# One load of the last head's values goes as three loads over 96, 20 and 12 rows

## The chip, the cores and the metric

The kernel runs on one core of a Trainium2 chip. The metric is the device time of one execution in microseconds. Before the change the median of three runs is 1369.03 us (1367.49 to 1369.67).

A core has engines that work side by side: TensorE (PE, with its weight loads as PEld), VectorE (DVE), ScalarE (ACT), GpSimd (POOL) and SyncE (SP). SP and ACT also issue DMAs. A DMA is carried out by up to sixteen DMA engines, which move its rows from the chip's memory (HBM) into the on-chip memory of 128 rows (partitions).

## The reference, cut to what matters

One token goes through two layers of attention over a long cache, each followed by a small MLP:

```
x = x + attention(layernorm(x))     # 32 heads, 8192 cached keys and values of 128 numbers
x = x + mlp(layernorm(x))           # 640 -> 1728 -> 640
x = x + attention(layernorm(x))     # the same cache and weights once more
x = x + mlp(layernorm(x))

q = x @ wq                          # per head: scores = q . k * 128**-0.5
p = softmax(scores);  o = p @ v     # over 8192 keys, then @ wo
```

Keys and values are float32: 4 MB of keys and 4 MB of values per head, 268 MB in all. Both layers read the same cache.

## The kernel before

The host lays keys and values out in one long array, `kv`, in the order in which they are read. A head is cut into units (`UNITS`, lines 41 to 53), each of which is one DMA. Most heads have two units, all keys and all values, of 4096 KB each. The heads at the ends of the layers are cut finer. Heads 0 and 31 have the units `HALVES[:2] + LAST`: two of keys with 2048 KB each, then four of values: blocks 0 and 1 (2048 KB, unit number 2), block 2 (1024 KB), three rows of block 3 (768 KB) and its last row (256 KB).

All units go through a ring in on-chip memory, 3496 x 8 numbers per row and 128 rows. `pump` (line 122) takes the next unit of the list `todo`, asks `place` (line 109) for room, and issues its load on SP (line 132). Where there is no room it stops, and is called again each time `release` (line 157) has freed a piece that was used. So loads go out in a fixed order, and each waits on SP until the instructions that read its place before are through. A unit of 2048 KB is 128 rows of 16 KB, one for each partition, and lies in `kv` row by row.

The first layer (0 in the code) goes through heads 0 to 31, the second (1 in the code) through heads 31 to 0. The ring still holds the last units of head 30 and all of head 31 when the first layer ends; the second layer starts with these and doesn't load them again. Four further units of the second layer are loaded into buffers that the first layer has just finished with (`load_beside`, line 142, on SP).

For a head PE makes the scores from the keys (`scores`, line 365), DVE takes their maximum (line 377), ACT the exponentials (line 384), PE turns them (line 392), and PE multiplies them by the values (`values`, line 426). Then the head's output is put together (`output`, line 440) and goes into the projection. Other small work of the layer is put between the pieces of a head by `side_work`: projections, queries of the next heads, and products of weights with weights.

In the last head of a layer the order matters most. Its keys' scores are mixed with the first MLP product (`hidden`, line 581). Values of blocks 0 and 1 come first, then another part of `hidden`, then blocks 2 and 3, then `output`. After that comes what remains of the MLP (`mlp`, line 759), which needs the head's output at once (line 762). In the first layer the loads beside and the next layer's start follow from it, in the second the result's store.

The DMAs of SP and ACT signal their end on semaphores, which the program hands out in turn. An instruction that reads a unit waits for the semaphore of its load.

Of the kernel before, what the change touches and what calls it, by code (L numbers as in the profile page):

```python
# [15 lines left out]
P = 128  # L16
# [34 lines left out]
] + HALVES[2:]  # L51
UNITS[28] = [("k", K_ALL[:1]), ("k", K_ALL[1:2])] + HALVES[1:]
UNITS[31] = HALVES[:2] + LAST
BESIDE = 4
DROPPED = {30: BESIDE}
RING = 3496
# [5 lines left out]
def wide(kind, piece):  # L62

    return 4 * piece[2] * (1 if kind == "k" else DH) // 8


def size(unit):
    return sum(wide(unit[0], piece) for piece in unit[1])
# [10 lines left out]
def decode_kernel(ctx: ExitStack, tc: tile.TileContext, x, kv, wq, wo, w1, w2, out):  # L79
    nc = tc.nc  # L80
# [12 lines left out]
    ring = consts.tile([P, 8 * RING], F32, name="ring")  # L93
# [5 lines left out]

    beside = todo[len(order) : len(order) + BESIDE]  # L100
    del todo[len(order) : len(order) + BESIDE]
    dram_at, o = {}, 0
# [6 lines left out]
    def place(layer, n):  # L109


        step = max(m for m in (8, 256, 512) if n % m == 0)
        low, high = (0, RING) if layer else ((3072, RING) if n == RING - 3072 else (0, 3072))
        at, best = low, None
        for a, m in sorted(live.values()) + [(high, 0)]:
            a = min(a, high)
            if a - at >= n and (best is None or a - at < best[1]):
                best = at, a - at
            at = max(at, -(-(a + m) // step) * step)
        return None if best is None else best[0]  # L120

    def pump():
        while todo:
            layer, u = todo[0]
            kind, pieces = unit = UNITS[u[0]][u[1]]
            n = size(unit)
            at = place(layer, n)
            if at is None:
                return
            todo.pop(0)  # L130
            o = dram_at[u]
            nc.sync.dma_start(
                ring[:, 8 * at : 8 * (at + n)],
                kv[o : o + 8 * P * n].rearrange("(p m) -> p m", p=P),
            )
            for t, piece in enumerate(pieces):
                m = wide(kind, piece)
                live[layer, u, t] = at, m
                at_of[layer, u, t] = ring, 8 * at
                at += m  # L140
# [16 lines left out]
    def release(L, u, t):  # L157
        if (L or u not in kept) and at_of[key(L, u, t)][0] is ring:
            del live[key(L, u, t)]
            pump()  # L160
# [23 lines left out]
    nc.sync.dma_start(xr, x)  # L184
    load_wq(0, nc.sync)
    pump()
    load_wo(0, nc.sync)

# [805 lines left out]
```

## Time and profile before

| | |
|---|---|
| median of the runs | 1369.03 us |
| the profiled execution, its own time | 1367.16 us |
| its span, first to last instruction | 1365.4 us |
| PE busy | 1009.0 us (74%) |
| DVE busy | 182.8 us (13%) |
| ACT busy | 113.2 us (8%) |
| bytes moved by DMA | 572.70 MB, 419 GB/s over the span |
| mean granted TensorE clock | 0.806 |

The span counts from the first to the last instruction; the execution's own time also has what lies around it. "Busy" sums the time in which an engine worked. The DMA share of a stretch is the mean busy share of the sixteen DMA engines. In a timeline row the two first numbers are start and duration in us, then come the engine, the line, the operation, what it writes and reads, and how many instructions are merged; a bracket names the idle time before the first of them and what ended it. A row of a windows table has the stretch, its length, the busy time (and instructions) of PE, PEld, DVE, ACT and POOL, the granted clock, the DMA share and the GB/s.

### The profile page before, as it was taken

The page shows a single profiled execution, that of the slowest core. Times are in us where ns is not written, and L with a number is a line of the kernel's source. Part 1 is how long each engine was busy: PE and PEld are TensorE (multiplying, and loading weights), DVE is VectorE, ACT ScalarE, POOL GpSimd, SP SyncE. Part 2 cuts the span into 40 slices and gives each one's busy share as a digit, 9 for nine tenths or more (in the row PEclk, how much of TensorE's full clock was granted, in tenths as well). Part 3 has the DMA queues.
Part 4 walks back from the last instruction along what each step waited for, and adds up shares of the span by engine and source line. Part 5 has one row for each costly group of instructions (what it writes and reads, how often), then busy time and mean ns, then how long its engine had stood idle before and what let it go on. Part 6 is the DMA issues. An engine that isn't in the chain of part 4 may idle for free.

```text
span 1365.4 us, 16727 instructions
## 1 busy us (share of the span) xinstructions
PE 1009.0 (74%) x7546; PEld 409.8 (30%) x7546; DVE 182.8 (13%) x696; ACT 113.2 (8%) x305; POOL 2.9 (0%) x10
## 2 busy tenths in 40 slices
PE   5564766877787777787888767676777787787778
PEld 2121312322333323343344322232222322223224
DVE  1010100111101101111122111110110101111112
ACT  0000000000101101111000100010100000000000
POOL 0000000000000000000000000000000000000000
PEclk9786867887878877888799987787788877787879
DMA  9999999999999999999979999999999999999995
GB/s 393 431 435 428 431 429 427 431 429 433 429 432 430 425 434 428 434 430 418 426 298 395 433 433 429 429 429 431 432 429 432 426 432 430 433 426 430 431 427 218
DMA packets 28736, 572.70 MB, mean 419 GB/s; under 512 B 3189, under 2 KB 3321, under 8 KB 5625
## 3 DMA queue, kind: packets, MB, share of 16 engines
q1 hardware_dynamic: 23912, 525.27, 90.0%
q10 hardware_dynamic: 4752, 46.37, 8.1%
q8 instruction: 59, 0.97, 0.3%
q14 instruction: 13, 0.10, 0.0%
HBM read 571.62 MB, written 0.00 MB: 419 GB/s over the span
## 4 chain that ended last, share of the span: by engine, by line
DMA 66%; PE 30%; DVE 2%; ACT 1%; issue 1%; SPq 0%; POOLq 0%; POOL 0%; ACTq 0%; DVEq 0%
DMA ring<-in_kv 66%; PE outs L426 11%; PE ps L365 10%; PE px L505 2%; PE pt L392 1%; ACT p L384 1%; PE px L311 1%; DVE h_t L377 1%; PE acc L581 1%; PE acc L331 1%; PE pm L412 1%; PE pm L452 1%; PE px L558 1%; PE px L538 0%; PE px L550 0%
## 5 line engine op out<-in xcount | busy, mean ns | idle before, releaser
L365 PE MATMUL ps<-ring,spread_q 128*32 128x512 f32 (+2 forms) x2064 | 319.9, 735 | 175.6 <-DMA ring<-in_kv 175.5
L426 PE MATMUL outs<-ring,pT 128*4 128x512 f32 (+2 forms) x2128 | 333.2, 776 | 47.0 <-DMA ring<-in_kv 46.7
L365 PEld LDWEIGHTS ps<-ring,spread_q 128*32 128x32 f32 x2064 | 62.0, 128 | 291.5 <-DMA ring<-in_kv 183.8
L426 PEld LDWEIGHTS outs<-ring,pT 128*4 128x4 f32 x2128 | 57.5, 101 | 255.1 <-issue 193.7
L377 DVE TENSOR_REDUCE h_t<-ps 128x1 f32<-128x512 f32 x64 | 44.3, 692 | 473.8 <-PE ps L365 473.6
L452 PE MATMUL pm<-h_t,p 128*128 128x1 f32 (+1 forms) x512 | 69.9, 258 | 34.6 <-DVE p L443 34.3
L452 PEld LDWEIGHTS pm<-h_t,p 128*128 128x128 f32 x512 | 64.6, 194 | 98.2 <-DVE p L443 97.2
L384 ACT ACTIVATE p<-ps,h_t 128x512 f32<-128x512 f32 x63 | 43.3, 687 | 578.7 <-DVE h_t L377 567.4
L392 PE MATMUL pt<-row_of,p 128*128 128x16 f32 x512 | 68.2, 265 | 22.7 <-ACT p L384 22.6
L443 DVE COPY p<-outs 128x256 f32<-128x256 f32 x62 | 26.3, 425 | 355.4 <-PE outs L426 355.4
L392 PEld LDWEIGHTS pt<-row_of,p 128*128 128x128 f32 x512 | 62.1, 191 | 34.6 <-ACT p L384 34.4
L405 PE MATMUL pm<-ident,h_t 128*128 128x128 f32 x128 | 31.1, 324 | 40.2 <-DVE h_t L377 40.2
L444 ACT COPY p<-outs 128x256 f32<-128x256 f32 x62 | 23.1, 372 | 454.5 <-DVE p L443 454.5
L505 PE MATMUL px<-w_t,wct 128*128 128x448 f32 (+1 forms) x80 | 46.8, 672 | 0.2 <-DVE wqc L527 0.2
L405 PEld LDWEIGHTS pm<-ident,h_t 128*128 128x128 f32 x128 | 19.0, 187 | 92.0 <-DVE h_t L377 89.6
L412 PE MATMUL pm<-h_t 128*128 128x1 f32 x128 | 27.7, 285 | 24.6 <-DVE h_t L409 24.6
L311 PE MATMUL px<-wq_t,ln_xc 128*32 128x128 f32 x630 | 31.1, 362 | 1.9 <-DMA wq_t<-in_wq 1.9
L311 PEld LDWEIGHTS px<-wq_t,ln_xc 128*32 128x32 f32 x630 | 26.7, 150 | 16.5 <-issue 13.6
L412 PEld LDWEIGHTS pm<-h_t 128*128 128x128 f32 x128 | 22.2, 217 | 30.8 <-DVE h_t L409 30.8
L331 PE MATMUL acc<-wo_t,o_cols 128*32 128x160 f32 x496 | 28.1, 382 | 0.0
L331 PEld LDWEIGHTS acc<-wo_t,o_cols 128*32 128x32 f32 x496 | 20.4, 144 | 18.7 <-issue 14.9
L505 PEld LDWEIGHTS px<-w_t,wct 128*128 128x128 f32 x80 | 13.9, 219 | 37.6 <-issue 36.5
(151 smaller groups left out, 344.3 us busy)
## 6 DMA issues: line engine op xcount, KB each, us to landing
ring<-in_kv SPq DMA_DIRECT2D x104, 4096.0 KB, 25.2
ring<-in_kv SPq DMA_DIRECT2D x29, 2048.0 KB, 23.0
wo_t<-in_wo ACTq DMA_DIRECT2D x14, 1280.0 KB, 17.5
wq_t<-in_wq ACTq DMA_DIRECT2D x13, 1280.0 KB, 17.3
ring<-in_kv SPq DMA_DIRECT2D x15, 1024.0 KB, 24.0
w_t<-in_w ACTq DMA_DIRECT2D x1, 4480.0 KB, 24.7
w_t<-in_w ACTq DMA_DIRECT2D x1, 4320.0 KB, 25.3
ring<-in_kv SPq DMA_DIRECT2D x3, 768.0 KB, 27.1
```

Of the source, the lines that this page charges most:

```text
L311: nc.tensor.matmul(pq[32 * j : 32 * j + 32, :DH], xc[:, c : c + 1].to_broadcast([P, 32]), weights_of(g, c, j), start=(c == 0), stop=(c == ...
L331: nc.tensor.matmul(acc[32 * g : 32 * g + 32, :DR], col.to_broadcast([col.shape[0], 32]), wt[:, g * DR : (g + 1) * DR], start=first, stop=last,
L365: nc.tensor.matmul(hd.ps[32 * g : 32 * g + 32, c : c + n], spread_q[:, 3 - r : 35 - r], tile_of[:, at + g * n : at + (g + 1) * n], start=f ...
L377: nc.vector.tensor_reduce(hd.nm, hd.ps, AX.X, ALU.max, negate=True)
L384: nc.scalar.activation(hd.p, hd.ps, AF.Exp, bias=hd.nm, scale=scale, accum_out=hd.l)
L392: nc.tensor.matmul(pt[:, 16 * b : 16 * b + 16], hd.p[:, b * P : (b + 1) * P], row_of.rearrange("p g r -> p (g r)"), start=True, stop=True,)
L405: nc.tensor.matmul(pt[:, :P], hd.nm.to_broadcast([P, P]), ident, start=True, stop=True)
L412: nc.tensor.matmul(pt[:, :1], hd.l.to_broadcast([P, P]), hd.wi, start=True, stop=True)
L426: nc.tensor.matmul((hd.out if r0 < 3 else hd.out_3)[32 * g : 32 * g + 4, r0:r1].rearrange("p r d -> p (r d)"), hd.pT[:, 4 * i : 4 * i + 4] ...
L443: nc.vector.tensor_copy(oc[:, :2], hd.out[:, :2])
L452: nc.tensor.matmul(pt[:, :n], oc[:, r], hd.w[:, r : r + 1].to_broadcast([P, n]), start=(r == 0), stop=(r == 3),)
L505: nc.tensor.matmul(pt[:, :n], wct[:, c], w1_t[:, c, f : f + n], start=(c == 0), stop=(c == NB - 1),)
```

## The change

The load of unit 2 of head 31 in the first layer, and of unit 2 of head 0 in the second, is issued as three DMAs one after the other on SP. They cover the partitions 0 to 95, 96 to 115 and 116 to 127. The bytes, their place in `kv` and their place in the ring stay the same, and so do all other loads. The instructions that read the unit now depend on three DMAs.

```diff
+UNEVEN = [(31, 2), (0, 2)]
+SHARES = [(0, 96), (96, 116), (116, 128)]
...
-            nc.sync.dma_start(
-                ring[:, 8 * at : 8 * (at + n)],
-                kv[o : o + 8 * P * n].rearrange("(p m) -> p m", p=P),
-            )
+            for p0, p1 in SHARES if u == UNEVEN[layer] else [(0, P)]:
+                nc.sync.dma_start(
+                    ring[p0:p1, 8 * at : 8 * (at + n)],
+                    kv[o + 8 * p0 * n : o + 8 * p1 * n].rearrange("(p m) -> p m", p=p1 - p0),
+                )
```

## The prediction

> **What bounds the kernel now.** The page comes first: its span, its queues, and the chain of waits.
>
> ```profile
> span 1365.4 us, 16727 instructions
> DMA  9999999999999999999979999999999999999995
> ...
> q1 hardware_dynamic: 23912, 525.27, 90.0%
> ...
> q8 instruction: 59, 0.97, 0.3%
> ...
> DMA 66%; PE 30%; DVE 2%; ACT 1%; issue 1%; SPq 0%; POOLq 0%; POOL 0%; ACTq 0%; DVEq 0%
> ...
> ring<-in_kv SPq DMA_DIRECT2D x29, 2048.0 KB, 23.0
> ```
>
> The stream of keys and values bounds the kernel: the sixteen DMA engines are full but for two slices, the layer's border and the end. The changed load lies just ahead of each of these. One row of it, 16 KB, costs an engine 0.900 x 16 x 1365.4 us over 525.27 MB / 16384 B (32060 rows), so 0.613 us. I call this a row time. The same load is now eight row times per engine, 4.9 us.
>
> The second view is the windows at the end of the second layer, and the timeline beside them.
>
> ```profile
> core 0: us, PE busy (x) PEld busy (x) DVE busy (x) ACT busy (x) POOL busy (x), PEclk, DMA share, GB/s
> 1341.00:1345.00 4.00, 3.38 (x32) 1.04 (x36) 0.12 (x1) 0.00 (x0) 0.00 (x0) 1.00 0.99 411
> 1345.00:1347.00 2.00, 2.00 (x23) 0.89 (x15) 0.69 (x1) 0.78 (x2) 0.00 (x0) 1.00 0.82 339
> 1347.00:1349.00 2.00, 1.62 (x16) 1.29 (x18) 0.76 (x5) 0.29 (x1) 0.00 (x0) 1.00 0.58 242
> 1349.00:1351.00 2.00, 2.00 (x40) 0.99 (x36) 0.28 (x1) 0.00 (x0) 0.00 (x0) 1.00 0.46 189
> 1351.00:1352.00 1.00, 1.00 (x22) 0.50 (x18) 0.00 (x0) 0.00 (x0) 0.00 (x0) 1.00 0.24 84
> 1352.00:1353.00 1.00, 1.00 (x25) 0.37 (x15) 0.08 (x1) 0.00 (x0) 0.00 (x0) 1.00 0.00 0
> ```
>
> The engines don't finish together. The first fall silent at about 1345 and the last at 1352, and for 4 us (1347 to 1351) about half of them run. What is left at 1345 is 0.82 x 2 + 0.58 x 2 + 0.46 x 2 + 0.24 = 4.0 us of all sixteen, so evenly shared rows would land 3 us earlier. The halves differ by about 5 us, which is eight row times. Half as many engines move about half the bytes (189 GB/s at 0.46, 411 at 0.99): each runs at its own pace, and silence of the others doesn't speed it.
>
> ```profile
> 1348.68 0.11 PEld L426 LDWEIGHTS outs<-ring,pT 128*4 128x4 f32 x8
> 1348.68 1.91 PE L426 MATMUL outs<-ring,pT 128*4 128x384 f32 x32
> ...
> 1351.12 1.94 PE L426 MATMUL outs<-ring,pT 128*4 128x384 f32 x32
> ...
> 1351.77 0.35 PEld L426 LDWEIGHTS outs<-ring,pT 128*4 128x4 f32 x12 [0.19 <-issue]
> 1352.51 0.25 PEld L426 LDWEIGHTS outs<-ring,pT 128*4 128x4 f32 x8 [0.40 <-DMA ring<-in_kv]
> ```
>
> PE takes the changed unit (blocks 0 and 1 of the last head's values) at 1348.68 without a wait, and the rest of the head from 1351.12. Only the last eight weight loads wait, 0.40 us against 0.19 by issue alone, and the matmuls hardly notice: 1.94 us for 32 against 1.91. So PE and the last bytes arrive together. An earlier landing is worth at most 0.03 us here. A later one has a little cover: those last matmuls are 8 x 128 of the group's 16 x 384 + 16 x 128 columns, 0.24 us. They end at 1353.06, so they start at 1352.82, 0.3 us after their weights.
>
> The first layer ends alike:
>
> ```profile
> 699.00:701.00 2.00, 1.62 (x19) 1.29 (x22) 0.82 (x5) 0.30 (x1) 0.00 (x0) 1.00 0.57 230
> 701.00:703.00 2.00, 2.00 (x40) 0.93 (x36) 0.22 (x1) 0.00 (x0) 0.00 (x0) 1.00 0.49 200
> 703.00:705.00 2.00, 2.00 (x37) 0.93 (x29) 0.14 (x1) 0.00 (x0) 0.00 (x0) 1.00 0.21 83
> ```
>
> ```profile
> 700.62 1.91 PE L426 MATMUL outs<-ring,pT 128*4 128x384 f32 x32
> ...
> 703.06 1.94 PE L426 MATMUL outs<-ring,pT 128*4 128x384 f32 x32
> ...
> 704.35 0.35 PEld L426 LDWEIGHTS outs<-ring,pT 128*4 128x4 f32 x8 [0.29 <-DMA ring<-in_kv]
> ...
> 706.93 0.94 PE L581 MATMUL acc<-mix,c_ol 128*32 128x448 f32 x8 [0.25 <-DVE c_ol L459]
> ```
>
> Half of the engines run for 4 us, and the last weights come 0.4 us ahead of their matmuls (705.00 - 0.24 - 704.35). The output of the head, the mixed weights (line 762) and the next layer's first loads hang on these matmuls, so a delay here passes on whole.
>
> **The change part by part.** *Rows per engine.* How many engines share a load can be counted in the queues. The first answer is a stretch with one load of 128 rows on queue 10, the second is the last 3 us, which hold only the store of four rows.
>
> ```profile
> q10 hardware_dynamic: 144, 1.31, 17.4%
> ...
> wo_t<-in_wo ACTq DMA_DIRECT2D x1, 1280.0 KB, 17.2
> ```
>
> ```profile
> q1 hardware_dynamic: 8, 0.00, 0.4%
> ...
> out<-xr SPq DMA_DIRECT2D x1, 2.5 KB
> ```
>
> 128 rows make 144 packets, 128 and 16 end marks; four rows make 8, four and 4 marks. So engines take equal shares, up to sixteen of them. Then 96 rows go six each; 20 rows go two each on ten engines (more can't share them evenly) and 12 rows one each on twelve; at the least four engines serve each, as with the store. If both begin at the same engine, ten engines get 6 + 2 + 1 = 9 rows, two get 7 and four get 6, where all had 8. [...]
>
> *What that moves, if a row keeps its price.* Eight engines are late and only six get lighter, so two late ones at least take a ninth row: the last landing moves between -0.61 us (two early ones among the late take it) and +0.61. Behind the cover of 0.3 and 0.4 us, PE loses up to 0.3 + 0.2 us in the two layers; a gain ends at 0.03 in each. I take +0.3 us together.
>
> *What a row costs in the new loads.* Until now every load covers the same 128 rows in the same shares, so the trace can't say whether the 0.613 us belongs to the engine or to the rows it writes. It does say that the engine isn't all: queue 8 brings 16 KB of instructions to another place in 0.003 x 16 x 1365.4 / 59 = 1.1 us (0.9 to 1.3 by the rounding of 0.3%). If rows own the lanes, sixteen lanes of eight rows, then the new loads crowd them. With neighbouring rows in a lane, rows 0 to 95 lie in twelve lanes: eight row times there instead of six. Rows 96 to 115 lie in 2.5 lanes, and 116 to 127 in 1.5: up to eight row times each, while twelve engines stand in line. From above that is 8 + 8 + 8 - 8 = 16 row times, +9.8 us, when nothing overlaps. From below, the early engines pass through each lane before the late ones arrive (they are eight row times ahead), and only the ninth row is left, +0.6 us. Nothing in the trace is nearer to one end, so I take the middle, +5.2 us in each layer. Less the cover that is 4.9 and 4.8, together +9.7 us.
>
> [...]
>
> *Issue and waits.* Two more issues in each layer:
>
> ```profile
> 1324.63 1.37 SPq L132 DMA_DIRECT2D ring<-in_kv  x3
> ```
>
> ```profile
> 684.70 0.11 PEld L426 LDWEIGHTS outs<-ring,pT 128*4 128x4 f32 x8 [3.42 <-DMA ring<-in_kv]
> ...
> 693.96 0.33 SPq L146 DMA_DIRECT2D wqc<-in_kv  x1
> ```
>
> ```profile
> 1332.77 0.11 PEld L426 LDWEIGHTS outs<-ring,pT 128*4 128x4 f32 x8 [1.98 <-DMA ring<-in_kv]
> ```
>
> Three issues take SP 1.37 us, so two more are 0.9 us, 20 us before the data is needed; the stream queued ahead hides them. The program hands its loads eight semaphores in turn, so a load waits for the eighth before it. The last small load will now wait for the last values of the head before, which land by 1332.77 (684.70 in the first layer), instead of going out by 1326. The earliest engine runs dry only at 1345, 12 us later; without that cover the cost would be the delay, 7 us. Behind it on SP stand the loads of line 146 in the first layer, the first of which goes out at 693.96 anyway, and in the second layer the store at the end. PE waits for three loads rather than one ahead of line 426. In the plain case they land before 1348.68, and the checks are at 0 to 0.1 us.
>
> The sum is 1367.16 us (the profiled execution's own time; its span is 1365.4) + 9.7 = 1376.9. The median of the runs shown is 1.87 us above that execution, so 1369.03 + 9.7 = 1378.7 us.
>
> **The rivals.** *Engines own the lanes.* Then the time is 1369.03 + 0.3 = 1369.3 us, no change. For it speaks that each engine keeps its pace when half are silent; against it, the 1.1 us of the instructions. It is the rival on the other side. It decides where a row in the new loads still takes 0.61 us.
>
> *Few engines.* If 20 and 12 rows go on four engines each, these take 6 + 5 + 3 = 14 rows, six more: +3.7 us, less the cover 3.4 and 3.3, so 1375.7 us. The store's four marks allow it; equal shares over sixteen speak against it.
>
> *Relief.* The 1.87 us between profiled and other executions could be waits for the late engines at both ends. If two rows less (1.2 us a layer) reached PE whole, the time would be 1369.03 - 2.4 = 1366.6 us. It decides only if PE in those runs waits over 0.6 us at each end for the last bytes, and if at most the two earliest of the eight late engines get a ninth row; here it waits 0.03.
>
> **How the numbers follow.** A measurement of this kernel tells about 0.2%, 2.7 us, from no change. Crowded lanes get 0.56: the trace leaves both owners open, and the price of instructions leans to the place written. Of this 0.52 is over 2.7 us and 0.04 under. Few engines get 0.06, all slower. Engine lanes get 0.32, no change. Relief gets 0.06, 0.04 of it faster and 0.02 within. So 0.58 slower, 0.38 the same, 0.04 faster. The likeliest case alone reaches from 1372 us to its upper bound, 1369.03 + 19.6 - 0.7 = 1388 us. The range of 8 in 10 takes in the engine lanes, 1367.5 to 1384 us.
>
> **What would show it.** Queue 1 has 23912 packets. With 16, 10 and 12 marks a layer has 22 more, 23956 in all; with 16, 4 and 4 it is 23928. Crowded lanes show as a DMA share near 1 with far fewer GB/s than 411 between 1340 and 1355 and around 700, the last weight loads of line 426 waiting some 5 us, and the first of them (at 1348.68 now) waiting too. Engine lanes show the same 411 GB/s, and a share that falls from 0.99 to 0 in 6 to 8 us. The forecast falls if both ends keep their 1.94 us matmul groups. The few-engine case shows a long tail at a share of about 0.25.

## The result, and the profile after

The changed kernel takes 1388.97 us (median of five runs, 1386.55 to 1393.16) against 1368.12 us before on the same chip (1367.49 to 1369.67). The ratio is 1.0148, with a 95% interval of 1.0136 to 1.0161. The forecast was 1378.7 us and the range ended at 1384.0 us: the direction was right, and the loss is more than twice the size.

From the page of the changed kernel: span, DMA activity in 40 slices, queues, and the chain of waits.

```profile
span 1384.7 us, 16734 instructions
DMA  9999999999999999999979999999999999999995
GB/s 394 432 430 433 426 430 432 430 426 431 431 430 431 430 429 432 428 425 425 399 193 402 428 433 431 427 431 430 434 430 428 429 432 428 433 431 430 430 410 129
...
q1 hardware_dynamic: 23956, 525.27, 90.2%
...
q8 instruction: 59, 0.97, 0.3%
...
DMA 70%; PE 26%; DVE 2%; ACT 1%; issue 0%; SPq 0%; POOLq 0%; POOL 0%; ACTq 0%; DVEq 0%
```

Queue 1 moves the same 525.27 MB with 44 packets more. The time of its packets rises from 0.900 x 1365.4 to 0.902 x 1384.7 us of each of the sixteen engines, so by 20.1 us (give or take 1 us by rounding). That is as much as the whole loss: the bytes are the same, and their transfer has become dearer.

The windows show where. Here is the end of the first layer, after (columns: stretch, length, busy time and instructions of PE, PEld, DVE, ACT and POOL, granted clock, DMA share, GB/s).

```profile
680.00:685.00 5.00, 4.62 (x24) 2.15 (x28) 0.83 (x5) 0.00 (x0) 0.00 (x0) 0.50 1.02 433
685.00:690.00 5.00, 3.68 (x28) 1.34 (x23) 0.58 (x2) 0.37 (x1) 0.00 (x0) 0.91 1.08 344
690.00:695.00 5.00, 3.55 (x34) 1.29 (x34) 0.33 (x2) 0.00 (x0) 0.00 (x0) 0.77 0.95 200
695.00:700.00 5.00, 3.24 (x28) 1.52 (x28) 0.38 (x2) 0.00 (x0) 0.00 (x0) 0.50 1.05 231
700.00:705.00 5.00, 4.04 (x22) 1.17 (x26) 0.00 (x0) 0.00 (x0) 0.00 (x0) 0.50 0.95 200
705.00:710.00 5.00, 4.40 (x36) 2.37 (x28) 1.44 (x5) 1.07 (x3) 0.00 (x0) 0.86 0.91 219
```

The end of the second layer, after, in the same columns:

```profile
1341.00:1345.00 4.00, 1.47 (x16) 0.32 (x16) 0.00 (x0) 0.00 (x0) 0.00 (x0) 0.96 1.02 434
1345.00:1350.00 5.00, 3.87 (x24) 2.07 (x20) 0.58 (x2) 0.37 (x1) 0.00 (x0) 0.50 1.08 324
1350.00:1355.00 5.00, 4.49 (x36) 1.91 (x28) 0.72 (x4) 0.00 (x0) 0.00 (x0) 0.50 0.97 208
1355.00:1360.00 5.00, 3.14 (x16) 0.63 (x20) 0.00 (x0) 0.00 (x0) 0.00 (x0) 0.50 0.99 225
1360.00:1365.00 5.00, 5.00 (x43) 2.13 (x35) 0.95 (x2) 0.78 (x2) 0.00 (x0) 0.83 0.99 212
```

For some 20 us at each end all sixteen engines are busy (DMA share 0.91 to 1.05) and move half of what they did: 200 to 231 GB/s where the first stretch of each table has 433 and 434. That is another picture than the tail of the kernel before, where half of the GB/s went with half of the share (189 GB/s at 0.46). At half pace a stretch of 20 us moves what 10 us would.

What PE sees of it, in the timelines. Before, the last keys and the matmul that follows the head's end:

```profile
694.50 1.06 PE L365 MATMUL ps<-ring,spread_q 128*32 128x512 f32 x8
1342.56 0.16 PEld L365 LDWEIGHTS ps<-ring,spread_q 128*32 128x32 f32 x8 [1.14 <-DMA ring<-in_kv]
1354.98 0.94 PE L581 MATMUL acc<-mix,c_ol 128*32 128x448 f32 x8 [0.25 <-DVE c_ol L459]
```

After, the same places and the values between them (the lines of the code stand four further down):

```profile
700.96 1.94 PE L369 MATMUL ps<-ring,spread_q 128*32 128x512 f32 x8 [2.21 <-DMA ring<-in_kv]
711.14 1.91 PE L430 MATMUL outs<-ring,pT 128*4 128x384 f32 x32 [1.36 <-issue]
715.10 1.06 PE L430 MATMUL outs<-ring,pT 128*4 128x384 f32 x16 [0.45 <-DMA ring<-in_kv]
718.09 0.94 PE L585 MATMUL acc<-mix,c_ol 128*32 128x448 f32 x8 [0.25 <-DVE c_ol L463]
...
1358.57 1.94 PE L369 MATMUL ps<-ring,spread_q 128*32 128x512 f32 x8 [1.77 <-DMA ring<-in_kv]
1367.05 1.91 PE L430 MATMUL outs<-ring,pT 128*4 128x384 f32 x32 [0.73 <-DMA ring<-in_kv]
1371.00 1.09 PE L430 MATMUL outs<-ring,pT 128*4 128x384 f32 x16 [0.44 <-DMA ring<-in_kv]
1374.02 0.95 PE L585 MATMUL acc<-mix,c_ol 128*32 128x448 f32 x8 [0.25 <-DVE c_ol L463]
```

The matmul of `hidden` that follows the head starts at 718.09 in place of 706.93 us in the first layer, 11.2 us later. In the second it starts at 1374.02 in place of 1354.98, 19.0 us later, of which 7.9 us are new. The span grows by 19.3 us. The delay reaches PE in part ahead of the changed unit: the last keys, an unchanged load, come 6.5 us later in the first layer (694.50, 700.96), and 4.8 us on top of the first layer's delay in the second (1342.56, 1358.57). Between the keys and the values PE itself is slower too: eight matmuls of scores take 1.94 us where they took 1.06, with a granted clock of 0.50 in place of 1.00. The end isn't set by that, as the last sixteen matmuls of the values still wait for a DMA in both layers (0.45 and 0.44 us).

### The profile page after: what moved, and what is told of

Read it like the earlier page. It is cut to its first block, busy times and chain, and to the rows that moved or that the text cites. A ratio compares the mean times of both kernels' runs of the same rounds, so it can differ in the third digit from the quotient of the medians.

```text
span 1384.7 us, 16734 instructions
## 1 busy us (share of the span) xinstructions
PE 1021.4 (74%) x7546; PEld 413.9 (30%) x7546; DVE 182.6 (13%) x696; ACT 113.2 (8%) x305; POOL 2.9 (0%) x10
## 3 DMA queue, kind: packets, MB, share of 16 engines
q1 hardware_dynamic: 23956, 525.27, 90.2%
## 4 chain that ended last, share of the span: by engine, by line
DMA 70%; PE 26%; DVE 2%; ACT 1%; issue 0%; SPq 0%; POOLq 0%; POOL 0%; ACTq 0%; DVEq 0%
DMA ring<-in_kv 70%; PE outs L430 10%; PE ps L369 9%; PE px L509 2%; PE pt L396 1%; ACT p L388 1%; DVE h_t L381 1%; PE px L562 1%; PE acc L335 1%; PE pm L416 1%; PE px L315 1%; PE px L554 0%; PE pm L456 0%; DVE pT L404 0%; PE pt L335 0%
## 5 line engine op out<-in xcount | busy, mean ns | idle before, releaser
L430 PE MATMUL outs<-ring,pT 128*4 128x512 f32 (+2 forms) x2128 | 338.7, 788 | 55.5 <-DMA ring<-in_kv 53.9
L396 PE MATMUL pt<-row_of,p 128*128 128x16 f32 x512 | 71.8, 273 | 21.9 <-ACT p L388 21.6
L396 PEld LDWEIGHTS pt<-row_of,p 128*128 128x128 f32 x512 | 65.6, 200 | 33.9 <-ACT p L388 33.8
```

What stands on the lines that cost most here:

```text
L396: nc.tensor.matmul(pt[:, 16 * b : 16 * b + 16], hd.p[:, b * P : (b + 1) * P], row_of.rearrange("p g r -> p (g r)"), start=True, stop=True,)
L430: nc.tensor.matmul((hd.out if r0 < 3 else hd.out_3)[32 * g : 32 * g + 4, r0:r1].rearrange("p r d -> p (r d)"), hd.pT[:, 4 * i : 4 * i + 4] ...
```

## The experiments

The theory is the prediction's own: a lane into the on-chip memory belongs to the rows written there, and loads of neighbouring rows crowd the lanes. The lanes are the author's assumption and stand in no view; the runs can only test what would follow from them. The rivals: what an additional load or wait costs by itself, the uneven shares of the engines, the place that is read, and for the size of the loss, whether it goes by the bytes that are split or by the distance between early and late engines. The ratios are against the kernel before on the same chip, with 95% intervals; a loss in us is the ratio's excess times 1368 us. The edits are to the changed kernel, and some show only the lines that matter.

### Three loads, no rows split

`cols` cuts the same unit into three loads by columns: each covers all 128 rows, and the bytes are as with 96, 20 and 12 rows.

```diff
+COLUMNS = [(0, 3072), (3072, 3712), (3712, 4096)]
-            for p0, p1 in SHARES if u == UNEVEN[layer] else [(0, P)]:
+            for c0, c1 in COLUMNS if u == UNEVEN[layer] else [(0, 8 * n)]:
                 nc.sync.dma_start(
-                    ring[p0:p1, 8 * at : 8 * (at + n)],
-                    kv[o + 8 * p0 * n : o + 8 * p1 * n].rearrange("(p m) -> p m", p=p1 - p0),
+                    ring[:, 8 * at + c0 : 8 * at + c1],
+                    kv[o : o + 8 * P * n].rearrange("(p m) -> p m", p=P)[:, c0:c1],
                 )
```

> The same two loads (unit 2 of the last heads) go as three loads each, cut by columns (12288, 2560 and 1536 bytes of each row) instead of by rows: all 128 rows in each, so every engine keeps its own eight rows. Lanes owned by rows: nothing is crowded, 1368.1 us within 0.5 us. Cost of the extra loads themselves (their issue, end marks, semaphores and the waits on them): all of the loss stays, 1386 to 1391 us.

Measured 1368.93 us against 1368.33, a ratio of 1.0003 (0.9994 to 1.0013). Two more issues, waits and end marks cost nothing that shows; cutting by rows does.

### One layer alone

```diff
-UNEVEN = [(31, 2), (0, 2)]
+UNEVEN = [(31, 2), None]        # first
+UNEVEN = [None, (0, 2)]         # second
```

> The three loads by rows in the first layer only. Lanes owned by rows: the loss of the first layer alone, by the later time of its last matmuls about 11 us: 1377 to 1383 us. If one layer's skew feeds the other, so that the losses don't add: either nearly the whole 20 us or nearly none.

> The three loads by rows in the second layer only. Lanes owned by rows: the rest, about 8 us: 1374 to 1379 us, so that this loss and that of the first layer alone make up the 20.3 us. If the second layer lost only because the first had spread its engines: under 1371 us.

`first` takes 1377.97 us, 1.0069 (1.0052 to 1.0086), and `second` 1378.06 us, 1.0072 (1.0057 to 1.0087). That is 9.4 and 9.9 us, together 19.3 of the 20.3 us. Within their intervals the two losses add up, and each is what the prediction had as its upper bound, 9.8 us.

### Even shares: halves

```diff
-SHARES = [(0, 96), (96, 116), (116, 128)]
+SHARES = [(0, 64), (64, 128)]
```

> Two loads of 64 rows instead of 96, 20 and 12: four rows for each engine in each, so every engine still has eight rows and none a ninth. Uneven shares of the engines as the cause: no change, 1368.1 us within 0.5 us. Lanes owned by rows: each half has eight lanes for sixteen engines, 8 + 8 - 8 row times at most, +4.9 us a layer less 0.3 us of cover: 1372 to 1378 us.

Measured 1387.96 us, 1.0142 (1.0127 to 1.0157), so 19.4 us, 9.7 in each layer. The expectation of 1372 to 1378 us was missed. By equal shares, which the end marks of the changed kernel bear out (16, 10 and 12 for its three loads), every engine has eight rows here as before the change, so the ninth row has no part in the loss. The end of the second layer with halves:

```profile
1340.00:1345.00 5.00, 4.45 (x26) 1.67 (x26) 0.93 (x6) 0.41 (x3) 0.00 (x0) 0.74 0.99 423
...
1350.00:1355.00 5.00, 3.28 (x25) 0.92 (x25) 0.33 (x2) 0.00 (x0) 0.00 (x0) 0.76 0.97 213
1355.00:1360.00 5.00, 3.01 (x24) 1.42 (x20) 0.38 (x2) 0.00 (x0) 0.00 (x0) 0.50 0.95 202
1360.00:1365.00 5.00, 3.70 (x20) 1.10 (x24) 0.00 (x0) 0.00 (x0) 0.00 (x0) 0.50 1.03 240
```

It is the same half pace at a full share: 202 to 240 GB/s at 0.95 to 1.03, where the first stretch has 423 at 0.99. Every engine counts as busy all the time, and a row takes about twice as long. The windows show this pace and not its cause.

### A smaller unit, and one in mid-stream

`tiny` splits the last unit of the head, one row of block 3 with 256 KB, and `middle` a unit of 4096 KB in the middle of each layer.

```diff
-UNEVEN = [(31, 2), (0, 2)]
+UNEVEN = [(31, 5), (0, 5)]      # tiny
+UNEVEN = [(16, 1), (15, 1)]     # middle
```

> The shares 96, 20 and 12 on the last unit of each layer (one row of block 3, 2 KB for each of the 128 rows) in place of unit 2, an eighth of its bytes. Loss in proportion to the bytes written out of place: an eighth of 10 us a layer, less the cover of 0.3 us, 0 to 2 us in all: 1368 to 1370.5 us. Loss by time, all engines at half pace from when the first engine enters the split load until the last one leaves it (they are 5 to 7 us apart): 3 to 6 us a layer, 1374 to 1380 us.

> The shares 96, 20 and 12 on the values of head 16 in the first layer and of head 15 in the second (4096 KB, twice the bytes) in place of the last heads' unit 2. Crowding that costs the stream itself: twice the loss per layer or nearly, 15 to 20 us each, 1395 to 1410 us. A loss that belongs to the ends of the layers only, where nothing can be caught up: under 1372 us.

`tiny` takes 1369.64 us, 1.0008 (0.9997 to 1.002), 1.1 us for both layers (2.7 at most). So the loss isn't a fixed price of about 10 us per split load, nor does it last for as long as the engines are apart (3 to 6 us a layer were expected for that). `middle` takes 1406.56 us, 1.0276 (1.0255 to 1.0296), 37.8 us, 18.9 in each layer: twice the bytes of the change, about twice the loss. In the first layer it shows so:

```profile
380.00:390.00 10.00, 5.58 (x52) 2.55 (x52) 0.00 (x0) 0.59 (x1) 0.00 (x0) 0.66 0.96 213
390.00:400.00 10.00, 5.37 (x42) 3.17 (x38) 1.81 (x7) 1.34 (x4) 0.00 (x0) 0.96 1.01 191
400.00:410.00 10.00, 0.00 (x0) 0.00 (x0) 0.00 (x0) 0.00 (x0) 0.00 (x0) 0.50 0.93 228
410.00:420.00 10.00, 7.53 (x40) 2.04 (x40) 0.58 (x2) 0.37 (x1) 0.00 (x0) 0.67 1.00 428
```

Thirty microseconds at half pace cost fifteen at least, and nothing later makes up for it, though the layer's end is nearly 300 us away (the head's output is used at 706.93 before). The stream itself is what sets the time, so the layer's end isn't needed for a loss.

### Which rows go together

`quarters` makes four loads of 32 neighbouring rows. `alternate` makes two loads, one of the even and one of the odd rows.

```diff
+SHARES = [(0, 32), (32, 64), (64, 96), (96, 128)]       # quarters

+for q, step in ((0, 2), (1, 2)) if u == UNEVEN[layer] else [(0, 1)]:    # alternate
     nc.sync.dma_start(
+        ring[q:P:step, 8 * at : 8 * (at + n)],
+        kv[o : o + 8 * P * n].rearrange("(p m) -> p m", p=P)[q:P:step],
     )
```

> Unit 2 of the last heads as four loads of 32 rows, two rows for each engine in each. [...] Lanes of eight neighbouring rows: four lanes instead of eight, a row costs four row times, and the loss is about three times that of the halves, over 1410 us.

> Unit 2 of the last heads as two loads, the even rows and the odd rows, 64 each and four for each engine. [...] Lanes of eight neighbouring rows, with neighbouring rows going to one engine: each engine stays in its own lane, no loss, 1368 to 1370 us. [...]

`quarters` takes 1388.02 us, 1.0145 (1.012 to 1.017), the same as halves. `alternate` takes 1369.71 us, 1.0002 (0.9992 to 1.0013): nothing. Its end of the second layer has the old pace:

```profile
1340.00:1345.00 5.00, 4.40 (x50) 2.53 (x52) 0.38 (x2) 0.00 (x0) 0.00 (x0) 0.92 0.95 392
1345.00:1350.00 5.00, 4.62 (x56) 2.72 (x50) 1.73 (x6) 1.07 (x3) 0.00 (x0) 1.00 0.53 219
1350.00:1355.00 5.00, 4.75 (x66) 2.82 (x62) 0.91 (x3) 0.00 (x0) 0.00 (x0) 1.00 0.04 13
```

A load of 64 rows, half of the 128, isn't dear by itself, then: as neighbouring rows two such loads cost 1.0142, as alternating rows 1.0002. The loss of `halves` belongs to the neighbouring rows. But lanes of eight neighbouring rows, the prediction's own, don't survive, though they give no loss for `alternate`: with them 32 rows would meet four lanes and be slower than 64, which meet eight, and over 1410 us were expected. Measured are 1388.02 us for 32 neighbours and 1387.96 for 64. Whether other lanes would give all three results no run shows.

### Read or written

`source` stores the unit's even rows ahead of its odd ones, so that two loads read one contiguous half each, as halves do, and write alternating rows, as `alternate` does. Since the order in memory has changed, unit 2 of head 0 is loaded this way in the first layer too.

```diff
+            half = P // 2 * 8 * n
+            for q, step in ((0, 2), (1, 2)) if u in UNEVEN else [(0, 1)]:
                 nc.sync.dma_start(
+                    ring[q:P:step, 8 * at : 8 * (at + n)],
+                    kv[o + q * half : o + (q + 1) * half if step > 1 else o + 8 * P * n].rearrange(
+                        "(p m) -> p m", p=P // step
+                    ),
                 )
...
+            if (h, at) in UNEVEN:
+                block[:] = np.concatenate([block[0::2], block[1::2]])
```

> Unit 2 of heads 31 and 0 lies in memory as two blocks of 64 rows, the even rows and then the odd ones, and each block goes as one load to every second row on chip. So the reads are those of the two halves, 64 neighbouring rows each, and the writes are those of the alternating rows. The place written decides: no loss, 1368 to 1370 us. The place read decides: the loss of the halves, 1384 to 1392 us.

Measured 1369.27 us against 1369.65, 0.9999 (0.9988 to 1.0009). With halves' reads and `alternate`'s writes it behaves as `alternate` (1.0002) and not as `halves` (1.0142). Reading halves costs nothing here, so what decides is the place written.

### Combs

`combs` takes every second row, every fourth of the rest, and the other two eighths; `three` takes the last two eighths together as every fourth row.

```diff
+COMBS = [(0, 2), (1, 4), (3, 8), (7, 8)]    # combs: first row, step
+COMBS = [(0, 2), (1, 4), (3, 4)]            # three
+for q, step in COMBS if u == UNEVEN[layer] else [(0, 1)]:
     nc.sync.dma_start(
+        ring[q:P:step, 8 * at : 8 * (at + n)],
+        kv[o : o + 8 * P * n].rearrange("(p m) -> p m", p=P)[q:P:step],
     )
```

> Unit 2 of the last heads as four loads whose rows are spread over all partitions: every second row (64 rows), of the others every second (32), and of what is left the two halves by every eighth (16 and 16). As many loads as the quarters, and two of them as small as the change's 20 and 12 rows. If a load's rows are dealt to the engines in proportion to the load's own length, each engine stays in its own lane: no loss, 1368 to 1370 us. If small loads cost by their row counts: 1378 to 1392 us.

> Unit 2 of the last heads as three loads spread over all partitions: every second row (64 rows), and of the others twice every fourth (32 and 32). The four combs lost 4.8 us with two loads of 16 rows, every eighth row, in place of the last of these. [...] A cost of small loads or of steps between rows: the loss stays above half of it, 1372 us or more.

`combs` takes 1374.72 us, 1.0035 (1.0023 to 1.0047), 4.8 us; the expectation of no loss was missed. `three` takes 1368.53 us, 1.0005 (0.9993 to 1.0016), where 1372 us or more were expected for a cost of small loads or of steps. So one load of every fourth row is still free, and two of every eighth in its place are not. The end of the second layer with `combs`:

```profile
1340.00:1345.00 5.00, 3.94 (x44) 1.62 (x44) 0.71 (x4) 0.00 (x0) 0.00 (x0) 1.00 1.02 354
1345.00:1350.00 5.00, 3.63 (x22) 1.06 (x26) 0.00 (x0) 0.00 (x0) 0.00 (x0) 0.66 1.02 307
1350.00:1355.00 5.00, 4.62 (x56) 2.72 (x52) 1.73 (x6) 1.07 (x3) 0.00 (x0) 1.00 0.75 237
```

and with `three`:

```profile
1340.00:1345.00 5.00, 4.06 (x48) 1.61 (x44) 0.71 (x4) 0.00 (x0) 0.00 (x0) 1.00 0.99 417
1345.00:1350.00 5.00, 4.62 (x47) 2.37 (x39) 1.27 (x4) 1.07 (x3) 0.00 (x0) 1.00 0.83 346
```

With `combs` the pace falls to 354 and 307 GB/s at a share of 1.02. With `three` bytes and share fall together, as engines run out (346 at 0.83, 417 at 0.99). From `combs` to `three` step and size change together, one load of 32 rows for two of 16, so a price of small loads isn't separated from a price of the step. But the full share at 307 GB/s is the picture of `halves` again.

The expectation that `combs` would lose nothing assumed lanes owned by rows, and rows dealt to the engines in proportion to the load's length, so that each engine stays in its own lane. `alternate` and `three` agree with that (1.0002, 1.0005), `combs` doesn't (1.0035), and which engine writes which rows no run shows.

### How far the engines are apart

Why 16 row times and not 8? The traces also keep the signals with which the sixteen engines report the end of each load. From one load's first signal to the next one's is the time that the earliest engine takes, and from last to last that of the latest. Before, at the end of the second layer, a load of 2048 KB takes 4.9 us by both, and first and last are 6.2 us apart. In `halves`, the whole load ahead of the split one, the last keys, still takes 4.9 us by the first signals but 9.6 us by the last; in the changed kernel it is 4.9 and 9.5 us, in both layers. The two halves together take 9.6 us by the first and 8.0 us by the last. Block 2 behind them, a whole load of 1024 KB, takes 5.0 us by the first and 2.5 us by the last, and it took 2.5 and 2.4 us before.

So the whole loads beside a split one lose as well: the late engines in the load ahead of it (9.6 in place of 4.9 us) and the early ones in the load behind it (5.0 in place of 2.5 us). As a rule of thumb, an estimate from these signals, write L for the split load's row times per engine (8 here) and D for the distance between early and late engines. Each engine then loses L and once more the smaller of L and D. Before, at the layers' ends, the ninth signal of a load comes 4.5 to 5.0 us after the first, so D is about 8, and the sum is 16 row times, 9.8 us. In lock step, by the same estimate, it would be 8.

`start` halves a unit of keys right at the kernel's start, where the engines are still close: before, first and last signal of a load are 0.9 to 1.4 us apart there.

```diff
-UNEVEN = [(31, 2), (0, 2)]
-SHARES = [(0, 96), (96, 116), (116, 128)]
+UNEVEN = [(0, 1), None]
+SHARES = [(0, 64), (64, 128)]
```

> Two halves of 64 neighbouring rows for the second unit of the kernel's first head alone, 2048 KB, when the engines still run within 1 us of each other, and nowhere else. At the ends of the layers the halves cost 9.8 us each, where the engines are 5 to 7 us apart. If they cost that much because early engines crowd late ones and are crowded by them afterwards, the halves cost 8 row times here, 4.9 us: 1372 to 1375 us. If the cost does not hang on the spread: 9.8 us again, 1377 to 1380 us. If later loads make up for it: 1368 to 1370 us.

Measured 1376.07 us against 1369.65, 1.0047 (1.0033 to 1.0061): 6.4 us, 4.5 to 8.3. The median lies between the two ranges expected, 1372 to 1375 and 1377 to 1380 us; the interval holds 4.9 and excludes 9.8. Before and then `start`, in the same stretches:

```profile
12.00:15.00 3.00, 2.72 (x16) 0.68 (x16) 0.00 (x0) 0.00 (x0) 0.00 (x0) 1.00 1.05 449
15.00:20.00 5.00, 1.45 (x12) 0.20 (x8) 0.00 (x0) 0.00 (x0) 0.00 (x0) 0.91 0.98 416
20.00:25.00 5.00, 3.82 (x23) 1.22 (x15) 0.98 (x2) 1.07 (x3) 0.00 (x0) 0.75 0.99 422
25.00:30.00 5.00, 4.62 (x31) 1.58 (x30) 0.83 (x5) 0.00 (x0) 0.00 (x0) 0.66 1.05 429
```

```profile
12.00:15.00 3.00, 2.06 (x12) 0.68 (x16) 0.00 (x0) 0.00 (x0) 0.00 (x0) 1.00 1.04 213
15.00:20.00 5.00, 1.58 (x8) 0.00 (x0) 0.00 (x0) 0.00 (x0) 0.00 (x0) 1.00 0.95 218
20.00:25.00 5.00, 0.00 (x0) 0.00 (x0) 0.00 (x0) 0.00 (x0) 0.00 (x0) 0.56 0.99 260
25.00:30.00 5.00, 3.61 (x16) 0.69 (x16) 0.00 (x0) 0.00 (x0) 0.00 (x0) 0.50 0.98 410
```

The half pace, 213 to 260 GB/s, lasts about 12 us in place of 20, and from 25 us on the stream is at 410 GB/s again (429 before). By the signals the engines are 1.4 us apart before, first to last, and the unit takes 6.9 us longer by the first signals and 6.3 by the last. `both` tests the same from the other side: at the layers' ends it halves two neighbouring units of 2048 KB, the last keys and the values behind them.

```diff
-UNEVEN = [(31, 2), (0, 2)]
-SHARES = [(0, 96), (96, 116), (116, 128)]
+UNEVEN = [[(31, 1), (31, 2)], [(0, 1), (0, 2)]]
+SHARES = [(0, 64), (64, 128)]
-            for p0, p1 in SHARES if u == UNEVEN[layer] else [(0, P)]:
+            for p0, p1 in SHARES if u in UNEVEN[layer] else [(0, P)]:
```

> Halves of 64 rows for two loads in a row at each layer's end: unit 2, as in the halves, and unit 1 (keys) ahead of it. Every engine runs at half pace while the early engines are in their halves or the late ones in theirs, and the late ones are some 8 row times behind: for one unit 8 + 8 row times, for two 16 + 8, so 14.7 us a layer against 9.8: 1395 to 1401 us. A loss in proportion to the bytes cut (16 row times for each unit, whatever the engines' distance): 19.5 us a layer, 1404 to 1410 us.

Measured 1396.16 us against 1368.67, 1.0200 (1.0183 to 1.0217): 27.4 us, 13.7 in each layer (12.5 to 14.8). A loss by the bytes would be twice that of halves, 19.4. L + D is 16 + 8 row times, 14.7 us, less a cover of 0.3 to 0.4. The second of two neighbouring split loads costs 4 us, under half of the first.

The rule of thumb doesn't give `middle`, which is 16 row times long as well. Before, first and last signal of the loads there are 3.6 to 5.4 us apart, six to nine row times, so even by the outermost engines L + D is at most 25 row times, 15.3 us. Measured are 18.9 us a layer (17.4 to 20.2), which a loss by the bytes would give, and `both` speaks against that.

### Is an earlier landing worth anything?

`less` leaves work out: the unit's load brings only block 0, half of each row.

```diff
+            part = 8 * n // 2 if u == UNEVEN[layer] else 8 * n
             nc.sync.dma_start(
+                ring[:, 8 * at : 8 * at + part],
+                kv[o : o + 8 * P * n].rearrange("(p m) -> p m", p=P)[:, :part],
             )
```

> Unit 2 of the last heads is loaded in one DMA as before, but only its first half, block 0 (8 KB of each row); block 1 is left out and PE multiplies by what the ring held there. The last landing of each layer comes four row times (2.4 us) earlier. If PE is the bound from the last keys on, as the matmul groups of 1.94 us say, an earlier landing is worth under 0.1 us a layer: 1368 to 1369 us, as before. If the ends wait for the late engines: 1363 to 1366 us.

Measured 1369.03 us against 1369.65, 0.9999 (0.999 to 1.0009). The timeline and the last windows of `less`:

```profile
1346.62 1.91 PE L430 MATMUL outs<-ring,pT 128*4 128x384 f32 x32
1349.06 1.94 PE L430 MATMUL outs<-ring,pT 128*4 128x384 f32 x32
```

```profile
1340.00:1345.00 5.00, 4.63 (x48) 1.81 (x44) 0.69 (x1) 0.78 (x2) 0.00 (x0) 1.00 0.78 320
1345.00:1350.00 5.00, 4.62 (x71) 2.79 (x74) 1.04 (x5) 0.29 (x1) 0.00 (x0) 1.00 0.21 84
```

This execution, at 1365.20 us, is the fastest of its eleven, and its values start 2.06 us earlier than those of the profile before, but so do the last keys ahead of them (1340.51, 1342.56). Against its own matmuls the stream runs out some 2 us sooner, and the matmul groups keep their 1.91 and 1.94 us. In the kernel before, PE has nothing to gain from an earlier landing of these values, and all to lose from a later one.

## Why the prediction was wrong in size

**The bound.** Right: the stream sets the time, PE and the last bytes meet at the ends, and an earlier landing is worth nothing (`less`, 0.9999).

**Rows per engine.** Right to the packet: 23956 were forecast for 16, 10 and 12 engines and 23956 are there; in the trace 16, 10 and 12 engines signal the ends of the three loads. The few-engine rival, with 23928, has fallen.

**Issue and waits.** Right at nothing (`cols`, 1.0003).

**If a row keeps its price.** The rival of engine lanes, which held 0.32, has fallen: in the windows a full DMA share goes with 200 to 231 GB/s. Halves, with no ninth row, lose as much as the change (1.0142, 1.0148). The price of 16 KB on the queue of instructions, 1.1 us, pointed the right way; whether it has the same cause no run shows.

**What a row costs in the new loads.** Here the step failed. The prediction took crowded lanes as the likeliest and bounded a layer by 0.6 and 9.8 us, and measured are 9.4 and 9.9. What failed is the sentence on the lower end, that "the early engines pass through each lane before the late ones arrive" and only the ninth row is left. It took the engines' distance of eight row times for relief, and so pulled the term down to the middle, 5.2 us. The distance is no relief: the late engines lose while still in the whole load ahead (9.6 in place of 4.9 us for the last keys in `halves`), and the early ones later in the load behind (5.0 in place of 2.5 us for block 2). `start`, with little distance, loses 6.4 us, the layer's end 9.7. The term is near the upper end, 16 row times, and the time with it, 1388 us, is within 1 us of the measured one. That end was reached by another sum, three loads one after the other in lanes of eight neighbours, which `quarters` refutes (1388.02 us, where over 1410 were expected); that it comes to the measured size is chance. No run shows lanes or their number: what the runs show is half the pace at a full share, where blocks of neighbouring rows are written.

The expectation for `halves`, 8 row times or 4.9 us a layer, missed half of the loss (9.7): it took the load by itself, as in lock step, and not the whole loads that it holds up.

**What else it left out.** The delay was looked for in the last weight loads of line 426, which were to wait some 5 us. They wait less:

```profile
1358.56 0.20 PEld L369 LDWEIGHTS ps<-ring,spread_q 128*32 128x32 f32 x8 [3.27 <-DMA ring<-in_kv]
1370.99 0.11 PEld L430 LDWEIGHTS outs<-ring,pT 128*4 128x4 f32 x8 [0.73 <-DMA ring<-in_kv]
1371.68 0.11 PEld L430 LDWEIGHTS outs<-ring,pT 128*4 128x4 f32 x8 [0.58 <-DMA ring<-in_kv]
```

In these rows of the second layer after the change, the longest wait, 3.27 us, is for the last keys, which lie ahead of the changed load; the last two weight loads wait 0.73 and 0.58. The delay reaches back to loads in flight, for which the prediction had no term.

**What stays open.** Why blocks of neighbouring rows cost most (1.0142 to 1.0148), every eighth row some (1.0035) and alternating rows nothing (1.0002), no run shows, nor which engine writes which rows. That early and late engines lose time in whole loads beside the split one is shown (9.6 in place of 4.9 us, 5.0 in place of 2.5); how much of the total that is, is not settled. `middle` loses 18.9 us a layer and L + D gives 15.3 at most; it splits 96, 20 and 12 rows, and the longest load, and no run separates these. `start` differs from the layers' ends in its place too: another load was in flight beside it, and it splits keys. No version here is faster than the kernel before.

## What to carry to other kernels

A load of part of the rows isn't priced by its own bytes alone: where blocks of neighbouring rows were loaded, the whole loads beside them slowed down too (4.9 became 9.6 us for the last keys). If a large load has to be cut in a stream as full as this one, cut it by columns (1.0003) or into every second or fourth row (1.0002, 1.0005), not into blocks of neighbouring rows (1.0142 to 1.0148). And when a profile shows engines out of step, ask what the early ones hold up, before counting the distance as relief.

## What the runs showed of the hardware that was not expected

- The DMA share doesn't show the pace: it stays at 0.91 to 1.05 while the stream falls from 433 GB/s to between 200 and 231.
- One load of 2048 KB in each layer, of 525 MB in all, costs 1.4 to 1.5% of the time when it goes as two, three or four blocks of neighbouring rows (1.0142, 1.0148, 1.0145), and nothing as alternating rows (1.0002).
- 32 neighbouring rows do as badly as 64 (1.0145, 1.0142), and two loads of every eighth row cost (1.0035) where one of every fourth is free (1.0005).
- The sixteen engines of one stream drift apart: first and last end the same load 0.9 to 1.4 us apart near the kernel's start, 3.6 to 5.4 us in the middle of the layers and 6.2 to 6.7 us at their ends, all in the kernel before.
- Where the engines are close the loss is smaller (6.4 us against 9.7), and a second split load right behind the first costs under half of the first (4 us).
